# A causal convolution and a low-rank mixer: batch 0 in four half-row pieces, another warm-up, and one convolution a piece later

## The chip, the cores and the metric

The kernel runs on one core of a Trainium2 chip. A core has five engines that run side by side, each through its own queue in order: TensorE (PE, matrix products, with its weight loads shown as PEld), VectorE (DVE), ScalarE (ACT), GpSimd (POOL) and SyncE (SP). Matrix products land in PSUM, eight banks of 128 partitions x 512 float32 values; everything else lives in SBUF. Sixteen DMA engines move data between memory and SBUF.

The metric is the device time of one execution in microseconds. Before the change it is 331.23 us, the median of five runs (330.65 to 331.52).

## The reference

Eight batches of 4224 positions with 192 channels go through a causal convolution of 7 taps (softmax weights, one set for each of 8 heads of 24 channels), and then through a mixer: a rank-32 product over the positions is added, and a two-layer network over the channels with 768 hidden values is added to that.

```python
w = np.exp(weight - np.max(weight, axis=-1, keepdims=True))
w = w / (np.sum(w, axis=-1, keepdims=True) + 1e-09)
x_pad = np.concatenate([np.zeros((B, K - 1, D)), x], axis=1)
x_unf = x_pad[:, idx, :].reshape(B, S, K, H, group)      # idx = s + k
y = np.einsum('hk,bskhg->bshg', w, x_unf).reshape(B, S, D)

h = y.transpose(0, 2, 1) @ U @ V                         # over positions, rank 32
u = y + h.transpose(0, 2, 1)
out = u + np.maximum(u @ w_ch1, 0.0) @ w_ch2
```

## The kernel before

**Tiles.** The positions of a batch are 33 tiles of 128. x is held in blocks of 64 positions: partitions 0 to 63 (r = 0) hold the first 32 blocks, partitions 64 to 127 (r = 1) the last 34. The loads of x convert float32 to bfloat16 on the way and are issued by GpSimd (`x_part`, L76 to L82). The convolution is a matrix product with a band matrix: `conv` (L368) multiplies blocks of x by `band` (L181), two products for each block (itself and the block before), in 64 x 64 corners of the array, so that up to four run at once. It writes PSUM, and ACT (for r = 0) and DVE (for r = 1) copy the result to `y_sb` as bfloat16 (`evac`, L270 to L274). For batches 2 and later `conv32` (L334) does it with 32-row corners, and needs a copy of x shifted by 32 positions, `xb_sb`, that GpSimd makes in six steps (`x_shift`, L299 to L330).

**The head.** The band is built on the chip: GpSimd writes index tables (`iota`, L103 to L123), DVE makes a one-hot table `hot` of them, ACT and DVE the softmax weights `c_sb`, DVE the product `pr` of both (L223), in two halves of four heads, PE sums the seven taps through an identity (L231), and ACT copies the sums into `band` (L240). Meanwhile x of batch 0 is on its way in two pieces, each of both halves: `KP` (L86) cuts the tiles of each half at 13. PE runs 60 idle matmuls of zeros at the start and 30 ahead of the conv (`idle`, L170 and L688). Then PE does, in this order (L688 to L704): the conv of piece 0, head by head; `u_layout` (L276), which brings U into the order of the tiles with a selection matrix `Eq` and leaves `U_sb`; the transposes of y for the first group (`yT_part`, L542); the rank products of the first 26 tiles (`tt_mm`, L405, in four columns of 32 of the array); the conv of piece 1; a float32 product that adds up the four columns (`R4f`, L701); the rank products of the seven late tiles, each with U repeated four times, `U4_sb`, which DVE copies (L435); `tt_done` (L459), DVE's copy of the sum to `tt_sb`; `hT_part` (L558), which adds h to the transposed y and gives `uT`; and the first layer of the network, `w1` (L582, matmul in L590).

**The order of the rest.** Nothing is scheduled by a planner: each engine runs in the order in which the program is written, and a tile's reuse puts in the waits. `SLOTS` (L642 to L679) lists, slot by slot, which groups of eight tiles go through `w1` (36 matmuls each) and `w2` (L608, four pieces of 12 matmuls each), and ahead of which piece of `w2` the other work is put: `c3:0:3` is the conv of batch 3 for heads 0 to 2, `x4:3` the first three steps of the shifted copy of batch 4, `t3` the rank products of batch 3, `s3` their sum, `h10` group 10's mixer addition and transpose. For batches 3 and later the conv stands ahead of pieces 1, 2 and 3 (L669 to L671). The loads of batches 2 and later are held back until a given matmul of `w1` (`LOADS`, L682, `held`, L631).

**GpSimd's queue.** GpSimd issues all loads but one, in the order in which they are written: the first piece of x, index tables, U, the second piece, V for the first group, W1 in four parts, V in five, W2, x of batch 1, and then the four copies that make `band2` (L712). The completion signals of its loads go round over eight semaphores, so from the ninth load on an issue waits for the landing of the load eight before it. The first loads of x are the first two, U the next two, the second piece the fifth and sixth.

Of the kernel before, what the change touches and what calls it, by code (L numbers as in the profile page):

```python
# [7 lines left out]
ALU = mybir.AluOpType  # L8
# [6 lines left out]
def kernel(  # L15
# [10 lines left out]
    nc = tc.nc  # L26
# [59 lines left out]
    KP = [(0, 13), (13, NB1 // 2)]  # L86

    def x_piece(k):
        for r in range(2):
            k0, k1 = KP[k]  # L90
            k1 = min(k1, (NB0, NB1)[r] // 2)
            x_part(0, r, (1 - r if k == 0 else 2 * k0 + 1), 2 * k1 + 1)

    x_tile(0)
    x_piece(0)
# [5 lines left out]
    dif = cst.tile([P, BW], F32, name="dif")  # L101
    for r in range(4):
        nc.gpsimd.iota(  # L103
            dif[QB * r : QB * r + QB, :],
            pattern=[[1, BW]],
            base=0,
            channel_multiplier=-1,
            allow_small_or_imprecise_dtypes=True,
        )
    tap = cst.tile([P, KC], F32, name="tap")  # L110
    nc.gpsimd.iota(
        tap[:],
        pattern=[[-1, KC]],
        base=HW,
        channel_multiplier=0,
        allow_small_or_imprecise_dtypes=True,
    )

    fp = cst.tile([P, P], I32, name="fp")
    nc.gpsimd.iota(fp[:], pattern=[[1, P]], base=P, channel_multiplier=-1)  # L120

    efp = cst.tile([P, 4, P], I32, name="efp")
    nc.gpsimd.iota(efp[:], pattern=[[-1, 4], [1, P]], base=4 * P, channel_multiplier=-4)  # L123
# [11 lines left out]
    x_piece(1)  # L135


    V0_sb = cst.tile([32, 2 * GT * P], BF16, name="V0_sb")
# [28 lines left out]
    zz = cst.tile([P, 512], BF16, name="zz")  # L167
    nc.vector.memzero(zz[:])  # L168

    def idle(n, w):  # L170
        wps = bank()
        for _ in range(n):
            nc.tensor.matmul(  # L173
                out=wps[:, 0:w], lhsT=zz[:, 0:P], rhs=zz[:, 0:w], start=True, stop=True
            )

    idle(60, P)
# [3 lines left out]
    band = cst.tile([P, H, P], BF16, name="band")  # L181
    nc.vector.memzero(band[:])
    x_zero(0, nc.vector)
    hot = cst.tile([P, KC, BW], BF16, name="hot")
    nc.vector.tensor_tensor(
        out=hot[:],
        in0=dif[:].unsqueeze(1).to_broadcast([P, KC, BW]),
        in1=tap[:].unsqueeze(2).to_broadcast([P, KC, BW]),
        op=ALU.is_equal,
# [11 lines left out]
    nc.scalar.activation(e_sb[:], d_sb[:], ACT.Exp)  # L201
    ident = cst.tile([P, P], BF16, name="ident")
# [16 lines left out]
    HQ = H // 2  # L219

    def band_half(hh):
        pr = sml.tile([P, KC, HQ, BW], BF16, name="pr")
        nc.vector.tensor_tensor(  # L223
            out=pr[:],
            in0=hot[:].unsqueeze(2).to_broadcast([P, KC, HQ, BW]),
            in1=c_sb[:, :, HQ * hh : HQ * hh + HQ].unsqueeze(3).to_broadcast([P, KC, HQ, BW]),
            op=ALU.mult,
        )
        bp = bank()
        for d in range(KC):  # L230
            nc.tensor.matmul(  # L231
                out=bp[:, 0 : HQ * BW],
                lhsT=ident[:],
                rhs=pr[:, d, :, :],
                start=(d == 0),
                stop=(d == KC - 1),
            )
        for r in range(4):
            o = QB * (r % 2)
            nc.scalar.activation(  # L240
                out=band[QB * r : QB * r + QB, HQ * hh : HQ * hh + HQ, o : o + BW],
                in_=bp[QB * r : QB * r + QB, 0 : HQ * BW].rearrange("p (h t) -> p h t", h=HQ),
                func=ACT.Copy,
            )

    band_half(0)
    band_half(1)


    Eq = cst.tile([P, 4, P], BF16, name="Eq")  # L250
    nc.vector.tensor_scalar(
        out=efp[:], in0=efp[:], scalar1=P - 1, scalar2=None, op0=ALU.bitwise_and
    )
    nc.vector.tensor_scalar(
        out=Eq[:], in0=efp[:], scalar1=0.0, scalar2=None, op0=ALU.is_equal
    )
    nc.vector.tensor_scalar(
        out=fp[:], in0=fp[:], scalar1=R - 1, scalar2=None, op0=ALU.bitwise_and
    )
    R4f = cst.tile([P, P], F32, name="R4f")  # L260
    nc.vector.tensor_scalar(
        out=R4f[:], in0=fp[:], scalar1=0.0, scalar2=None, op0=ALU.is_equal
    )
    R4 = cst.tile([P, P], BF16, name="R4")
    nc.vector.tensor_copy(out=R4[:], in_=R4f[:])

# [9 lines left out]
    def u_layout():  # L276
        up = [bank() for _ in range(4)]
# [11 lines left out]
        for jj in range(4):  # L289
            evac(  # L290
                "AD"[jj % 2],
                U_sb[:, 0 : nb[jj], jj, :],
                up[jj][:, 0 : nb[jj] * R].rearrange("p (k r) -> p k r", r=R),
            )

# [38 lines left out]
    def conv32(b, h0, nh, engs):  # L334
# [5 lines left out]
        for n in range(nh):  # L340
# [3 lines left out]
            for cg in range(4):  # L344
                t, w, st = (
                    (xt[b], band[:, h, QB : 2 * QB], 1 + cg // 2)
# [21 lines left out]
    def conv(b, h0, nh, rs, engs, k0=0, k1=NT):  # L368
# [4 lines left out]
        pp = {r: bank() for r in rs}  # L373
        w = nh * GS
        for hh in range(nh):
            h = h0 + hh
            for halo in range(2):
                for r in rs:
                    for c in range(2):
# [5 lines left out]
                            lhsT=band[HB * r : HB * r + HB, h, HB * halo : HB * halo + HB],  # L385
# [42 lines left out]

    def tt_first(p, js, rest):


        U4_sb = cst.tile([P, sum(b - a for a, b in rest), 4, R], BF16, name="U4_sb")
        n = 0
        for a, b in rest:
            nc.vector.tensor_copy(  # L435
                out=U4_sb[:, n : n + b - a, :, :],
                in_=U_sb[:]
                .rearrange("p k j r -> p (k j) r")[:, a:b, :]
                .unsqueeze(2)
                .to_broadcast([P, b - a, 4, R]),  # L440
            )
            n += b - a
        p = tt_mm(0, js, p, 256)
        t = sml.tile([P, D], F32, name="tt_f", bufs=1)
        evac("A", t[:], p[:, 256 : 256 + D])
        return U4_sb, t

    def tt_more(p, U4_sb, rest):
        js = [j for a, b in rest for j in range(a, b)]
        for n, j in enumerate(js):  # L450
            nc.tensor.matmul(
                out=p[:, 0:D],
                lhsT=U4_sb[:, n, :, :].rearrange("p a r -> p (a r)"),
                rhs=yt[0][:, j, :],
                start=False,
                stop=(n + 1 == len(js)),
            )
# [84 lines left out]
    def yT_part(g):  # L542

        tp = [bank() for _ in range(3)]
        for c in range(3):
# [12 lines left out]
    def hT_part(g, tp, engs):  # L558

        uTt[g] = uts.tile([P, 4, 3, P], BF16, name="uT")  # L560
        for c in range(3):
            for hf in range(2):
                nc.tensor.matmul(
                    out=tp[c][HB * hf : HB * hf + HB, :],
                    lhsT=ttb[0][0:32, HB * c : HB * c + HB],
# [4 lines left out]
                )  # L570
            for n, eng in enumerate(engs):
# [90 lines left out]
    for k in range(5, 14):  # L662
# [3 lines left out]
        if k < 10:  # L666
# [21 lines left out]
    idle(30, P)  # L688
    for h in range(H):
        conv(0, h, 1, [0, 1], "AD", *KP[0])  # L690
    u_layout()
    yT = yT_part(0)
    jb = NB0 // 2
    rest = [(KP[1][0], jb), (jb + KP[1][0], NT)]
    ps0 = bank()
    U4_sb, tf = tt_first(
        ps0, list(range(KP[1][0])) + list(range(jb, jb + KP[1][0])), rest
    )
    for h in range(0, H, 4):
        conv(0, h, 4, [0, 1], "AD", *KP[1])  # L700
    nc.tensor.matmul(out=ps0[:, 0:D], lhsT=R4f[:], rhs=tf[:], start=True, stop=False)  # L701
    tt_more(ps0, U4_sb, rest)
# [7 lines left out]
    for r in range(4):  # L710
        q = slice(QB * r, QB * r + QB)
        nc.gpsimd.tensor_copy(  # L712
            out=band2[q], in_=band[q, :, HB * (r % 2) : HB * (r % 2) + QB]
        )
# [84 lines left out]
```

## Time and profile before

| what | value |
|---|---|
| median of five runs | 331.23 us (330.65 to 331.52) |
| the profiled execution | 331.23 us, its span 329.4 us |
| PE busy | 317.9 us, 97% of the span |
| DVE busy | 268.6 us, 82% |
| ACT busy | 170.9 us, 52% |
| POOL busy | 142.0 us, 43% |
| idle matmuls L173 | 90, 6.9 us busy |
| W1 matmuls L590 | 1188, 132.0 us busy |
| W2 matmuls L614 | 1584, 141.7 us busy |
| conv matmuls L381 of x 64x312 (piece 0) | 64, starting 11.43 to 15.3 us |
| first matmul of W1 | at 21.68 us |

All times in the profile are in microseconds from the start of the span, means of one instruction in nanoseconds. A line of the timeline gives start, length, engine, line of the program, operation, what is written and read, its shape, how many instructions were merged, and in brackets how long the engine was idle before and what ended the wait. Matmuls overlap, so a busy PE may still be waiting for part of the time; PEclk is the clock that a throttle granted, which was 1.00 through the span.

### The profile page before, as it was taken

Reading aid. Unit: us, or ns where it says so; the run is one execution under the profiler, and the core shown is the slowest. Engines: PE = TensorE matmul, PEld = TensorE weight load, DVE = VectorE, ACT = ScalarE, POOL = GpSimd, SP = SyncE. Lnnn points to the kernel's source line nnn. Section 1 sums busy time; section 2 is a strip of 40 time slices with the busy share of each in tenths; the row PEclk is TensorE's granted clock in tenths of the full one; section 3 lists DMA queues with packets and bytes.
Section 4 is the critical chain, followed back from the end, with each engine's and each line's share of the span. In section 5 each row is a group of like instructions: output and inputs, shape, how many; then the busy total and the mean of one; then the engine's idle time right before and its main releaser. Section 6 shows DMA issues by size and latency. Waiting matters only on the chain.

```text
span 329.4 us, 9736 instructions
## 1 busy us (share of the span) xinstructions
PE 317.9 (97%) x4072; PEld 223.8 (68%) x4072; DVE 268.6 (82%) x547; ACT 170.9 (52%) x351; POOL 142.0 (43%) x109
## 2 busy tenths in 40 slices
PE   6889999999999999999999999999999999999995
PEld 6655676567646845976874694587797487487495
DVE  5657999996985998798699789879897897896863
ACT  1658444563486098258619806842912912912910
POOL 8580229763995695969559599000000000000000
PEclk9999999999999999999999999999999999999999
DMA  8999995799999999799989969039659159249035
GB/s 100 192 167 167 158 213 144 143 190 178 240 194 182 163 173 190 172 223 195 183 192 191 182 160 224 19 105 237 76 113 277 45 128 240 67 115 270 1 123 169
DMA packets 122908, 53.54 MB, mean 163 GB/s; under 512 B 87760, under 2 KB 122832, under 8 KB 122864
## 3 DMA queue, kind: packets, MB, share of 16 engines
q1 hardware_dynamic: 84672, 38.18, 51.0%
q0 software_dynamic: 38192, 14.73, 39.3%
q8 instruction: 32, 0.52, 0.7%
q14 instruction: 12, 0.10, 0.1%
HBM read 29.49 MB, written 25.95 MB: 168 GB/s over the span
## 4 chain that ended last, share of the span: by engine, by line
PE 78%; POOL 8%; DMA 7%; DVE 3%; ACT 3%; issue 1%; POOLq 0%; DVEq 0%
PE ps L614 37%; PE ps L590 32%; DMA x_sb<-in_x_dram 7%; POOL xb_sb L318 5%; PE ps L352 3%; PE ps L496 3%; ACT rl_sb L601 2%; POOL x_sb L79 2%; PE ps L411 2%; DVE y_sb L274 2%; POOL xb_sb L306 1%; DVE rl_sb L603 1%; PE ps L381 0%; PE ps L467 0%; DVE uT L274 0%
## 5 line engine op out<-in xcount | busy, mean ns | idle before, releaser
L601 ACT ACTIVATE rl_sb<-ps 128x512 bf16<-128x512 f32 x235 | 125.3, 605 | 111.1 <-PE ps L590 107.8
L614 PE MATMUL ps<-W_sb,rl_sb 128*128 128x192 bf16 x1584 | 141.7, 247 | 0.2
L614 PEld LDWEIGHTS <-rl_sb 128*128 128x128 bf16 x1584 | 128.0, 98 | 13.4 <-issue 12.8
L590 PE MATMUL ps<-uT,W_sb 64*128 64x512 bf16 x1188 | 132.0, 377 | 0.8 <-DVE uT L274 0.8
L603 DVE TENSOR_SCALAR rl_sb<-ps 128x512 bf16<-128x512 f32 x161 | 104.3, 687 | 17.7 <-PE ps L590 17.4
L590 PEld LDWEIGHTS <-W_sb 64*128 64x128 bf16 x1188 | 64.3, 94 | 64.2 <-issue 5.0
L622 DVE TENSOR_TENSOR out_sb<-ps,u_sb 128x384 f32<-128x384 f32 (+1 forms) x133 | 70.1, 549 | 24.9 <-PE ps L614 24.5
L318 POOL COPY xb_sb<-x_sb 32x3072 bf16<-32x3072 bf16 (+1 forms) x24 | 67.6, 2824 | 0.7
L518 DVE TENSOR_TENSOR u_sb<-y_sb,ps 128x192 bf16<-128x192 bf16 (+1 forms) x168 | 66.2, 459 | 0.0
L306 POOL COPY xb_sb<-x_sb 128x3072 bf16<-128x3072 bf16 x12 | 32.7, 2742 | 30.0 <-PE ps L352 15.9
L272 ACT ACTIVATE y_sb<-ps 128x384 bf16<-128x384 f32 (+3 forms) x90 | 36.8, 503 | 10.9 <-PE ps L352 7.9
L79 POOL DMA_DIRECT2D x_sb<-in_x_dram x32 | 27.0, 851 | 27.2 <-PE ps L590 16.2
L274 DVE CAST y_sb<-ps 128x408 bf16<-128x408 f32 (+2 forms) x42 | 20.8, 547 | 4.1 <-PE ps L381 3.0
L496 PE MATMUL ps<-tt_sb,V_sb 32*128 32x192 bf16 x264 | 12.6, 247 | 0.8 <-DVE tt_sb L461 0.6
L352 PE MATMUL ps<-xb_sb,band 64*32 64x384 bf16 (+1 forms) x192 | 12.4, 332 | 0.8 <-POOL xb_sb L318 0.8
L352 PE MATMUL ps<-x_sb,band 64*32 64x384 bf16 x192 | 12.1, 333 | 0.0
L496 PEld LDWEIGHTS <-V_sb 32*128 32x128 bf16 x264 | 4.7, 92 | 8.2 <-issue 8.2
L352 PEld LDWEIGHTS <-band 64*32 64x32 bf16 x384 | 4.6, 90 | 5.2 <-issue 4.1
L381 PE MATMUL ps<-x_sb,band 64*64 64x312 bf16 (+3 forms) x192 | 7.2, 277 | 0.9 <-DMA x_sb<-in_x_dram 0.9
L173 PE MATMUL ps<-zz 128*128 128x128 bf16 x90 | 6.9, 251 | 1.2 <-DVE zz L168 1.2
L425 ACT ACTIVATE tt_hi<-ps 128x192 bf16<-128x192 f32 x7 | 2.3, 330 | 10.8 <-PE ps L411 10.8
L173 PEld LDWEIGHTS <-zz 128*128 128x128 bf16 x90 | 6.6, 116 | 1.2 <-DVE zz L168 1.2
(64 smaller groups left out, 71.9 us busy)
## 6 DMA issues: line engine op xcount, KB each, us to landing
out_dram<-out_sb SPq DMA_DIRECT2D x131, 192.0 KB, 2.9
x_sb<-in_x_dram POOLq DMA_DIRECT2D x14, 384.0 KB, 7.3
x_sb<-in_x_dram POOLq DMA_DIRECT2D x7, 432.0 KB, 7.7
x_sb<-in_x_dram POOLq DMA_DIRECT2D x7, 408.0 KB, 7.8
x_sb<-in_x_dram POOLq DMA_DIRECT2D x1, 648.0 KB, 10.2
x_sb<-in_x_dram POOLq DMA_DIRECT2D x1, 624.0 KB, 7.3
uT<-u_sb SPq DMA_TRANSPOSE x31, 4.4
W_sb<-in_moe_w_ch_dram POOLq DMA_DIRECT2D x2, 192.0 KB, 5.2
```

Of the source, the lines that this page charges most:

```text
L79: return nc.gpsimd.dma_start(out=xt[b][HB * r : HB * r + HB, s0:s1, :], in_=x[b, blk * HB : (blk + s1 - s0) * HB, :].rearrange("(j p) d -> ...
L272: nc.scalar.activation(out=out, in_=in_, func=ACT.Copy)
L274: nc.vector.tensor_copy(out=out, in_=in_)
L306: nc.gpsimd.tensor_copy(out=xbt[b][:, s0:s1, :], in_=xt[b][:, s0 + 1 : s1 + 1, :])
L318: nc.gpsimd.tensor_copy(out=xbt[b][q, s0:s1, :], in_=xt[b][q, s0:s1, :])
L352: nc.tensor.matmul(out=pp[r][QB * cg : QB * cg + QB, 0 : nk[r] * GS], lhsT=w[hr], rhs=t[hr, st : st + 2 * nk[r] - 1 : 2, hs], start=True, ...
L518: nc.vector.tensor_tensor(out=u_group(g)[:, i : i + n, :, hf, :], in0=yt[b][:, run[0] : run[0] + n, :].rearrange("p n (c k) -> p n c k", c=3),
L590: last = nc.tensor.matmul(out=pp[hf][:], lhsT=W1_sb[HB * hf : HB * hf + HB, c, m * P : (m + 1) * P], rhs=uTt[g][HB * hf : HB * hf + HB, :, ...
L601: nc.scalar.activation(out=rl[:, m, hf, :], in_=pp[hf][:], func=ACT.Relu)
L603: nc.vector.tensor_scalar_max(out=rl[:, m, hf, :], in0=pp[hf][:], scalar1=0.0)
L614: nc.tensor.matmul(out=cps[:, a * D : (a + 1) * D], lhsT=rlt[g][:, m, hf, (i + a) * P : (i + a + 1) * P], rhs=W2_sb[:, m, :], start=(m == ...
L622: nc.vector.tensor_tensor(out=o[:, 0:n, :].rearrange("p n (c k) -> p n c k", c=3), in0=cps[:, 0 : n * D].rearrange("p (n c k) -> p n c k", ...
```

## The change

It has four parts.

1. Batch 0 comes in four pieces of one half each: tiles 0 to 9 of the half r = 0, tiles 0 to 9 of r = 1, then r = 1 from 10 (7 tiles), then r = 0 from 10 (6 tiles). The first two go through the conv together, two heads at a time; the third and fourth by themselves, three heads at a time, into the four PSUM banks that `u_layout` used.
2. The warm-up is six idle matmuls of float32 and 512 columns (five at the start, one between the two band halves) in place of ninety of bfloat16 and 128 columns.
3. Both products `pr` of the band are made ahead of both sums, the band lies in two tiles, DVE copies the second half of it, the index tables are made with one `iota` each and per-quarter offsets `rq` that DVE adds, and `Eq` is made in one step. `U4_sb` and `R4` are copied by GpSimd, behind all issues of loads and ahead of x of batch 1; `band2` is made by eight copies. The rank products of the first 20 tiles come after the conv of the third piece, the transposes of y in columns 128 to 191 after the late rank products, and `hT_part` issues all its matmuls ahead of its copies.
4. In the slot of batch 3 the conv and what follows it (`x4:3`, `t3`, `s3`) stand one piece of `w2` later.

The diff, cut to its core:

```diff
-    KP = [(0, 13), (13, NB1 // 2)]
+    KP = [(0, 0, 10), (1, 0, 10), (1, 10, NB1 // 2), (0, 10, NB0 // 2)]
     def x_piece(k):
-        for r in range(2):
-            k0, k1 = KP[k]
-            k1 = min(k1, (NB0, NB1)[r] // 2)
-            x_part(0, r, (1 - r if k == 0 else 2 * k0 + 1), 2 * k1 + 1)
+        r, k0, k1 = KP[k]
+        x_part(0, r, (1 - r if k0 == 0 else 2 * k0 + 1), 2 * k1 + 1)
...
-    x_piece(0)
+    for k in range(2):
+        x_piece(k)
...
-    for r in range(4):
-        nc.gpsimd.iota(dif[QB * r : QB * r + QB, :], pattern=[[1, BW]], ...)
+    iota(dif[:], [[1, BW]], 0, -1)
...
-    x_piece(1)
+    for k in range(2, len(KP)):
+        x_piece(k)
...
-    zz = cst.tile([P, 512], BF16, name="zz")
+    zz = cst.tile([P, 512], F32, name="zz")
     nc.vector.memzero(zz[:])
+    rq = cst.tile([P, 2], F32, name="rq")
+    for r in range(4):
+        for n, v in enumerate((32.0, -128.0)):
+            nc.vector.memset(rq[QB * r : QB * r + QB, n : n + 1], v * r)
-    idle(60, P)
+    wps = bank()
+    def idle(n):
+        for _ in range(n):
+            nc.tensor.matmul(out=wps[:], lhsT=zz[:, 0:P], rhs=zz[:], start=True, stop=True)
+    idle(5)
...
+    nc.vector.tensor_scalar(
+        out=dif[:], in0=dif[:], scalar1=rq[:, 0:1], scalar2=None, op0=ALU.add
+    )
...
-        for r in range(4):
-            o = QB * (r % 2)
-            nc.scalar.activation(out=band[...], in_=bp[...], func=ACT.Copy)
+        for r in range(4):
+            o = QB * (r % 2)
+            evac("AD"[hh], bands[hh][...], bp[...])
     band_half(0)
+    idle(1)
     band_half(1)
...
-    idle(30, P)
-    for h in range(H):
-        conv(0, h, 1, [0, 1], "AD", *KP[0])
-    u_layout()
-    yT = yT_part(0)
-    ps0 = bank()
-    U4_sb, tf = tt_first(
-        ps0, list(range(KP[1][0])) + list(range(jb, jb + KP[1][0])), rest
-    )
-    for h in range(0, H, 4):
-        conv(0, h, 4, [0, 1], "AD", *KP[1])
-    nc.tensor.matmul(out=ps0[:, 0:D], lhsT=R4f[:], rhs=tf[:], start=True, stop=False)
-    tt_more(ps0, U4_sb, rest)
+    for h in range(0, H, 2):
+        conv(0, h, 2, [0, 1], "AD", *KP[0][1:])
+    work = [bank() for _ in range(4)]
+    u_layout(work)
+    o = 0
+    for js in late:
+        nc.gpsimd.tensor_copy(
+            out=U4_sb[:, o : o + len(js), :, :],
+            in_=U_sb[:]
+            .rearrange("p k j r -> p (k j) r")[:, js[0] : js[-1] + 1, :]
+            .unsqueeze(2)
+            .to_broadcast([P, len(js), 4, R]),
+        )
+        o += len(js)
+    nc.gpsimd.tensor_copy(out=R4[:], in_=R4f[:])
+    ps0 = bank()
+    yT = yT_part(0, (0, 1))
+    conv_piece(2, work[0:3])
+    tt_mm(0, piece_tiles(0) + piece_tiles(1), ps0, 256)
+    tf = sml.tile([P, D], F32, name="tt_f", bufs=1)
+    evac("A", tf[:], ps0[:, 256 : 256 + D])
+    conv_piece(3, [work[3], work[0], work[1]])
+    nc.tensor.matmul(out=ps0[:, 0:D], lhsT=R4f[:], rhs=tf[:], start=True, stop=False)
+    tt_late(ps0, late[0], 0, False, False)
+    tt_late(ps0, late[1], len(late[0]), False, True)
+    yT_part(0, (2,), yT)
     tt_done(0, ps0)
     hT_part(0, yT, "AD")
...
-        if k < 10:
+        if k == 5:
+            at = {
+                2: ["c3:0:3:AAD"],
+                3: ["c3:3:3:AAD"],
+                4: ["c3:6:2:A", "x4:3"],
+                5: [hs[0]],
+                6: ["t3"],
+                8: ["s3", hs[1]],
+                11: [hs[2]],
+            }
+        elif k < 10:
```

`late` holds the tiles of the third and fourth piece (26 to 32, then 10 to 15), and `tt_late` is the loop of `tt_more` for one of them.

## The prediction

> **What bounds the kernel now.** I read the page first, then the chain of waits in order of time, then the timeline of GpSimd (POOL) and of TensorE (PE), and last the waits of PE. The chain over the whole span says that PE is the bound:
>
> ```profile
> PE 78%; POOL 8%; DMA 7%; DVE 3%; ACT 3%; issue 1%; POOLq 0%; DVEq 0%
> ```
>
> The rest of the chain lies in two places, and the change touches both. One is the head, the first 22 us, up to the first W1 matmul (L590). The chain there (start, length, what):
>
> ```profile
> 2.38 10.23 DMA x_sb<-in_x_dram
> 12.65 0.47 PE ps L381 x6
> 13.14 2.44 DVE y_sb L274 x6
> ...
> 19.07 0.77 PE ps L451 x7
> ...
> 19.93 0.37 DVE tt_sb L461
> ...
> 20.35 0.42 PE ps L563 x2
> ...
> 21.68 1.08 PE ps L590 x6
> ```
>
> The first load of x holds everything to 12.65, then eight casts on VectorE (DVE), the rank products, `tt_sb` at 19.93, and the first W1 matmul at 21.68. From there PE runs with hardly a gap, so what the head gains or loses at `tt_sb` arrives at the end one to one. The other place is the conv of batch 3, where PE stands still once more, for GpSimd's last shifted copy, which ends at 99.41 (PE's timeline, then GpSimd's):
>
> ```profile
> 99.46 0.33 PE L352 MATMUL ps<-xb_sb,band 64*32 64x408 bf16 x1 [0.83 <-POOL xb_sb L318]
> ```
> ```profile
> 96.33 3.08 POOL L318 COPY xb_sb<-x_sb 32x3456 bf16<-32x3456 bf16 x1
> ```
>
> **Own time.** The profiled execution took 331.23 us, the median of the five runs; its span is 329.4, so 1.83 lie around it. I add changes to 331.23.
>
> **The conv of batch 3 a piece later.** One W2 piece more stands ahead of it on PE: twelve matmuls, 1.10 us on the chain. PE reached the conv at 98.30 and sat 0.83 from its second matmul on; with 1.10 ahead it arrives at 99.40 and finds the copy done at 99.41, so about 0.8 goes, leaving 0 to 0.05. PE and GpSimd both shift with the head, since GpSimd's chain is anchored on PE's held-back load at 61.78 (after 1.57 of waiting), so the relation holds. What is moved along: `x4:3`, `t3`, `s3`. The shifted copies of batch 4 may start when conv 3 ends, 103.53 before and about 103.5 after, and GpSimd then waits 3.21 us for PE at 115.88 anyway; that wait covers a piece. `t3` to `s3` stays two pieces apart, and the next group after `s3` (h11) is all batch 2. Cost nothing.
>
> **The head until the conv.** x_tile 0 now comes as 20, 21, 14 and 12 blocks in four loads instead of 26, 27, 6 and 8. The data rate is steady at 188 to 194 GB/s from 5 us on, in order of issue: the first two loads together (1272 KB) landed at 12.6; now they are 984 KB, 288 KB or 1.55 us less, so about 10.9 (a shorter descriptor issue gives 0.15 more). One iota instead of four saves some 0.6 us of GpSimd, the band no longer waits for it: DVE's products `pr` (1.26 us each) end near 6.9 and 8.1 instead of 7.93 and 9.15, in spite of eight memsets of `rq` (0.1 each at most) and a `zz` of twice the size (0.49 by the band's row, not 0.27). DVE evacuates the second band half (four at about 0.28, after ACT's 288 ns row) and makes `Eq`; both lie before 11.5. The conv of pieces 0+1 is four evacuations on each of ACT and DVE (480 elements, about 0.58 and 0.65, between the rows of 384 and 512), not eight of 312, so 2.6 on DVE for 3.21.
>
> Idle matmuls: before, 90 of bf16. The windows of their line alone show what they do:
>
> ```profile
> 3.00:4.00 1.00, 1.00 (x12) 1.00 (x11) 1.00 0.75 54
> 4.50:5.50 1.00, 1.00 (x21) 1.00 (x20) 1.00 1.52 177
> ```
>
> The columns are time, PE and weight-load busy with counts, PEclk, DMA. PEclk says 1.00 throughout, but the number of 128-column matmuls in a microsecond doubles after 4.3. So PE starts at half pace (about 107 ns each) and opens 3.1 us after the first matmul. No float32 matmul of this size is in the trace; L701 (192 columns) gives 0.52 us on the chain for its two halves, 1.4 for 512. [...]
>
> PE's line then: conv 10.9 to 12.6, u_layout held by DVE's second cast to 12.9 and done at 13.4, `U_sb` out at about 14.9, third piece 14.1 to 15.3 (its load lands near 14.0), 20 rank matmuls to 15.95, fourth piece (load at 15.7) to 17.0, R4f to 17.4. **Were that all, the thirteen late rank matmuls (81 ns each) would end at 18.75 and `tt_sb` begin at 18.85 instead of 19.93: 1.1 saved.**
>
> The other reorderings cost nothing there: `hT_part` issues its six matmuls before its evacuations, which wait for the same two matmuls as before; the third and fourth piece write into the four banks of u_layout, whose evacuations are counted above.
>
> **What is late next: U4_sb.** It moved from DVE (L435, 352 and 282 ns) to GpSimd, and in GpSimd's order it comes after all load issues, the W2 weights' included. GpSimd before:
>
> ```profile
> 14.77 1.13 POOL L153 DMA_DIRECT2D V_sb<-in_moe_V_dram  x2
> 16.12 1.08 POOL L153 DMA_DIRECT2D V_sb<-in_moe_V_dram  x2 [0.22 <-issue]
> 17.19 0.58 POOL L160 DMA_DIRECT2D V_sb<-in_moe_V_dram  x1
> 17.76 0.86 POOL L164 DMA_DIRECT2D W_sb<-in_moe_w_ch_dram  x1
> 18.61 0.21 POOL L74 MEMSET x_sb<- 64x96 uint32 x1
> ```
>
> The third V issue (16.12) reuses the semaphore of the last x load, so it waits for that landing (issued at 7.35, 8.5 us, 15.85). x and U are the same bytes in total as before, at the same rate, so that landing stays, 0.15 earlier at best. Then four issues: 0.54+0.54+0.58+0.86 = 2.52. GpSimd is free at 18.45, as it was at 18.62. The copies then are 128 x 896 and 128 x 768. Their price by the nearest rows:
>
> ```profile
> L306 POOL COPY xb_sb<-x_sb x12: 2742/2742/2745, 48.1 to 190.8; 128x3072 bf16<-128x3072 bf16 x12
> L308 POOL COPY xb_sb<-x_sb x6: 500/500/501, 54.0 to 193.6; 32x384 bf16<-32x384 bf16 x6
> L712 POOL COPY band<-band x4: 386/393/398, 22.2 to 23.5; 32x256 bf16<-32x256 bf16 x4
> ```
>
> From 384 to 3072 elements the slope is 0.83 ns, with 0.18 fixed (256 gives 0.39, which fits): 0.93 and 0.82. [...] At DVE's rate (0.634 us for 896 elements, 0.71 ns) the pair would be 1.2; by the rows 1.75. I take the rows: same engine, same dtype, only the four-fold repeat is new. So the second copy is ready at 18.45+1.75+0.08 = 20.3 (20.0 with DVE's rate and an early landing, 20.6 with 10% more for the repeat).
>
> PE works seven late matmuls on the first copy from 19.45, waits, and does the last six from 20.4: 0.73 (7 took 0.81), ends 21.1, `tt_sb` at 21.2 instead of 19.93. **The head is 1.2 us longer, from 0.9 to 1.6**, not 1.1 shorter. Behind the waiting late matmuls on PE lie the transposes of the third 64 columns (8 matmuls, 0.3, which fit under the `tt_sb` cast of 0.36), hT and W1. After `tt_sb` the steps to W1 are the same, so W1 starts at 22.9.
>
> On GpSimd, R4 (about 0.3) and x of batch 1 are queued behind the copies: its four issues start at 20.6 instead of 18.73, and eight band2 copies of 0.29 take the place of four of 0.39, so it ends near 26.5 instead of 24.1. Its next issue waited for PE until 32.69 (8.56 idle), so that is covered; batch 1's loads, 8 us each, land by 32 and are used at 41.15. SP's queue has nothing new.
>
> PE's new idle stretch, 17.4 to 19.45, is 2.0 us. The longest in the trace that kept the full pace is 1.77 (6.26 to 8.03; band matmuls of 152 columns then took 67 ns each). [...] If it fell, the 0.83 of hT and 4.3 of W1 would cost some 1.5; I take zero.
>
> **Sum**: 331.23 + 1.2 - 0.8 = 331.6, with 0.9 to 1.6 and 0.75 to 0.83: 331.3 to 332.1. A measurement can tell about 0.2%, 0.66 us, from no change, so the likeliest case is within it: the head's gain is eaten by a copy in a queue, and the conv's gain pays most of that back.
>
> **Rivals.** *The copy is not the bound* (chance 0.11): GpSimd gets through its issues two microseconds sooner, because the last load lands sooner or its wait falls away. Against it: same bytes, same rate, an issue order that puts the copies last. Then 331.23 - 1.1 - 0.8 = 329.3. *The clock does not open* (0.08): float32 zeros are no activity for the gate. [...] It decides as soon as PE's line is more than 2.2 late, the slack under the copy; slower, 331.23 + 3.4 - 0.8 = 333.8. For it: no float32 stream is in the trace; against: zeros in bf16 did open it. *The batch 3 wait stays* (0.08), because GpSimd slips with its longer list: 331.23 + 1.2 = 332.4; against it stand the 8.56 and 1.57 of slack. The likeliest has 0.73.
>
> **Chances and range.** Likeliest 0.73, of which 0.58 within 0.2%, 0.13 above, 0.02 below. Slower: 0.13 + 0.08 + 0.08 = 0.29; faster 0.02 + 0.11 = 0.13; same 0.58. The range from 330.0 to 332.8 takes in the likeliest and the third rival and leaves out 0.19.
>
> **What would show it.** The two U4 copies on GpSimd start near 18.5 and end near 20.3, straight after the W2 issue; PE's late matmuls wait for GpSimd twice, some 2 us and then 0.4; `tt_sb` near 21.2, first W1 near 22.9. First conv matmul of the second half near 10.9. No wait for xb_sb at the conv of batch 3, and W1 to end 0.8 shorter. I am wrong if the copies end before 18, if conv starts after 13, or if the end moves by another amount than `tt_sb` less 0.8.

## The result, and the profile after

The changed kernel takes 331.73 us, the median of 43 runs (330.15 to 335.07), beside 331.08 us for the kernel before in 80 runs. The medians are 0.65 us apart; the ratio worked out from all runs is 1.0024, 95% interval 1.0009 to 1.0038, so the loss is small but clear of no change. The forecast of 331.6 was 0.13 below the median.

The profiled execution of the changed kernel tells another story than the median: it took 330.61 us (span 328.8), which is 0.62 *less* than the profiled execution of before. Its chain of waits in the head, in order of time (start, length, what):

```profile
1.47 7.29 PE ps L174 x10
...
10.12 0.48 PE ps L237 x7
...
10.62 0.30 DVE band L259
...
11.96 0.48 DVE Eq L286
...
12.89 1.23 DVE y_sb L259 x2
...
18.25 0.52 PE ps L717 x2
18.77 0.62 PE ps L682 x7
...
19.40 0.69 PE ps L682 x6
...
20.18 0.37 DVE tt_sb L437
...
21.93 1.08 PE ps L568 x6
```

`tt_sb` starts at 20.18, where before had 19.93, and the first W1 matmul at 21.93 instead of 21.68: the head is 0.25 us longer, not 1.2. Ahead of the late rank matmuls (L682) no wait of GpSimd's is left on the chain. The load queue and the two `U4_sb` copies stand in GpSimd's timeline (the copies write `U4_sb` from `U_sb`; the trace calls both U_sb):

```profile
15.05 1.19 POOL L149 DMA_DIRECT2D V_sb<-in_moe_V_dram  x2 [0.98 <-DMA x_sb<-in_x_dram]
16.23 0.52 POOL L156 DMA_DIRECT2D V_sb<-in_moe_V_dram  x1
16.73 0.88 POOL L160 DMA_DIRECT2D W_sb<-in_moe_w_ch_dram  x1
17.66 1.69 POOL L701 COPY U_sb<-U_sb 128x896 bf16<-128x896 bf16 x2
```

The order is the one forecast: third V issue held by x, then the issues, then the copies, 1.69 us for the pair (forecast 1.75). But the third V issue comes at 15.05, where before had 16.12, so the copies start at 17.66, not 18.45. PE on the other hand is late: five float32 idle matmuls end at 8.76. The second half of the band is therefore summed only by 10.6, DVE's copies of it and DVE's `Eq` end at 12.4 (forecast 11.5), and DVE's casts of `y_sb`, for which `u_layout` waits, start at 12.89; so PE reaches the late rank matmuls at 18.6 (forecast 17.4). The weight loads show how little it then waits, in brackets, for each of the copies:

```profile
18.64 0.53 PEld L682 LDWEIGHTS <-U_sb 128*128 128x128 bf16 x7 [0.16 <-POOL U_sb L701]
19.40 0.45 PEld L682 LDWEIGHTS <-U_sb 128*128 128x128 bf16 x6 [0.24 <-POOL U_sb L701]
```

The second place is the conv of batch 3, first in PE's timeline, then in GpSimd's:

```profile
97.45 2.15 PE L592 MATMUL ps<-W_sb,rl_sb 128*128 128x192 bf16 x24
99.54 0.35 PE L355 MATMUL ps<-xb_sb,band 64*32 64x384 bf16 x2
```
```profile
81.09 2.74 POOL L309 COPY xb_sb<-x_sb 128x3072 bf16<-128x3072 bf16 x1 [3.17 <-DMA x_sb<-in_x_dram]
...
95.40 3.08 POOL L321 COPY xb_sb<-x_sb 32x3456 bf16<-32x3456 bf16 x1
```

The conv starts without a wait, as forecast. But its shifted copy ended at 98.48, 0.93 earlier than before, because the chain of copies hangs on the landing of x of batch 3 (3.17 us of waiting), not on PE. Without the move PE would have come to the conv 1.10 earlier, at 98.44, and would have waited for next to nothing. The sum of the profiled execution closes: 331.23 + 0.25 (head) - 0.83 (wait gone) = 330.65, measured 330.61.

So the profile has a gain of 0.6 and the median a loss of 0.65. What separates them is in the list of all executions, each with its mean granted clock of TensorE:

| executions | clock 0.997 and up | 0.991 to 0.996 | below 0.991 |
|---|---|---|---|
| before (39 runs beside the first experiments) | 26, median 330.65 us | 13, 332.29 us | none |
| after (43 and the profiled one) | 25, 330.61 us | 7, 332.64 us | 12, 334.11 us |

At full clock the medians of the two kernels are 0.04 us apart. The means of all these executions are 331.18 and 332.02; without those below 0.991, of which the kernel before has none, the mean of after is 331.24. So nearly the whole difference, 0.8 on the mean, comes from them. The experiments ask where and why the clock falls.

### The profile page after: what moved, and what is told of

Its sections match the earlier page's. It is cut to its first block, busy times and chain, and to the rows that moved or that the text cites. A ratio compares the mean times of both kernels' runs of the same rounds, so it can differ in the third digit from the quotient of the medians.

```text
span 328.8 us, 9589 instructions
## 1 busy us (share of the span) xinstructions
PE 320.3 (97%) x3994; PEld 221.1 (67%) x3994; DVE 269.2 (82%) x553; ACT 170.4 (52%) x345; POOL 144.0 (44%) x113
## 4 chain that ended last, share of the span: by engine, by line
PE 91%; DVE 5%; ACT 3%; issue 0%; DVEq 0%
PE ps L592 41%; PE ps L568 37%; PE ps L355 3%; PE ps L472 3%; PE ps L174 2%; ACT rl_sb L579 2%; PE ps L417 2%; DVE y_sb L259 1%; DVE rl_sb L581 1%; PE ps L385 1%; DVE u_sb L494 1%; PE ps L682 0%; DVE out_sb L600 0%; DVE band L259 0%; PE ps L443 0%
## 5 line engine op out<-in xcount | busy, mean ns | idle before, releaser
L581 DVE TENSOR_SCALAR rl_sb<-ps 128x512 bf16<-128x512 f32 x161 | 104.4, 687 | 17.7 <-PE ps L568 17.4
L257 ACT ACTIVATE y_sb<-ps 128x384 bf16<-128x384 f32 (+4 forms) x88 | 37.4, 512 | 10.7 <-PE ps L355 7.8
L259 DVE CAST y_sb<-ps 128x408 bf16<-128x408 f32 (+4 forms) x38 | 20.2, 578 | 1.6 <-PE ps L385 1.5
L355 PE MATMUL ps<-xb_sb,band 64*32 64x384 bf16 x192 | 12.1, 332 | 0.0
L174 PE MATMUL ps<-zz 128*128 128x512 f32 x12 | 8.4, 855 | 1.5 <-DVE zz L164 1.5
L385 PE MATMUL ps<-x_sb,band 64*64 64x240 bf16 (+3 forms) x192 | 8.0, 276 | 0.4 <-DVE band L259 0.4
L385 PEld LDWEIGHTS <-band 64*64 64x64 bf16 x192 | 6.0, 106 | 2.2 <-issue 1.2
```

The source lines that it names most:

```text
L257: nc.scalar.activation(out=out, in_=in_, func=ACT.Copy)
L355: nc.tensor.matmul(out=pp[r][QB * cg : QB * cg + QB, 0 : nk[r] * GS], lhsT=w[hr], rhs=t[hr, st : st + 2 * nk[r] - 1 : 2, hs], start=True, ...
L581: nc.vector.tensor_scalar_max(out=rl[:, m, hf, :], in0=pp[hf][:], scalar1=0.0)
```

## Experiments

Three things were to be told apart. *The copy*: `U4_sb` in GpSimd's queue holds the late matmuls, and PE's wait there lets the clock fall. *The warm-up*: six float32 matmuls are a thin warm-up, and the clock falls for that. *The slot*: the move of the conv is worth 0.8. Each ratio is to runs of the kernel before on the same chip; their median was 330.94 us for the first four experiments, 331.06 for the next three, and 330.78 for the last, which ran on another chip.

### The changed kernel once more

No edit.

> The changed kernel unchanged. The profiled execution was 0.6 us shorter than the one of before, yet the median of its runs is 0.65 us longer, and its runs with a mean granted clock of 0.999 lie near 330.4 to 331.9 while those with 0.994 and 0.988 lie near 332.6 and 334.1. Theory 'clock': the difference is made by executions in which PE's clock falls back; they show again as a group near 332.6 and one near 334.1, about half of all, and a profile of one would show PEclk below 1 for 3.5 or 7 us somewhere in the first 30 us. Theory 'copy': every execution is longer by the wait for U4_sb; then the times form one group near 331.7.

Measured: 332.84 us (22 runs, 330.32 to 335.08), ratio 1.0044 (1.0018 to 1.0069). Ten executions at clock 0.997 and up have a median of 330.71, the three from 0.991 to 0.996 one of 332.85, and the nine below 0.991 one of 334.09. The three groups are the same as in the table above to 0.2 us; the median alone moves with the share of the groups (here it falls on the small middle group). The profiled execution was again one at full clock (0.997, span 328.6), with the copies at 17.57.

### The changed kernel with the warm-up of before

```diff
-    zz = cst.tile([P, 512], F32, name="zz")
+    zz = cst.tile([P, 512], BF16, name="zz")
...
-            nc.tensor.matmul(out=wps[:], lhsT=zz[:, 0:P], rhs=zz[:], start=True, stop=True)
+            nc.tensor.matmul(
+                out=wps[:, 0:P], lhsT=zz[:, 0:P], rhs=zz[:, 0:P], start=True, stop=True
+            )
-    idle(5)
+    idle(60)
...
     band_half(0)
-    idle(1)
     band_half(1)
+    idle(30)
```

> The changed kernel with the warm-up of before: 60 idle matmuls of bfloat16 at the start and 30 between the band and the conv. Theory 'clock': the low-clock groups go or shrink to what before has, and the median falls by about 1 us below the changed kernel's, to 330.2 to 330.7. Theory 'copy': the late rank matmuls wait for the same copies, so the same median as the changed kernel within 0.4 us.

Measured: 333.68 us (10 runs), ratio 1.0071 (1.0040 to 1.0101). Seven of ten executions are below 0.991; the other three have a median of 332.0. The theory of the warm-up falls: with the fuller warm-up the clock falls more often, not less. PE's and GpSimd's timelines of this profile (335.23 us, clock 0.984), then windows over all its lines (time, length, busy and count of PE, PEld, DVE, ACT, POOL, then the granted clock, DMA share, GB/s):

```profile
17.06 0.59 PE L719 MATMUL ps<-tt_f,R4f 128*128 128x192 f32 x2
19.26 2.26 PE L684 MATMUL ps<-y_sb,U_sb 128*128 128x192 bf16 x13 [1.61 <-POOL U_sb L703]
```
```profile
15.79 1.08 POOL L149 DMA_DIRECT2D V_sb<-in_moe_V_dram  x2 [1.77 <-DMA x_sb<-in_x_dram]
18.28 1.70 POOL L703 COPY U_sb<-U_sb 128x896 bf16<-128x896 bf16 x2
```
```profile
17.00:18.00 1.00, 0.65 (x7) 0.30 (x2) 0.59 (x1) 0.48 (x2) 1.00 (x2) 1.00 1.27 194
18.00:19.00 1.00, 0.00 (x0) 0.00 (x0) 0.00 (x0) 0.00 (x0) 0.96 (x2) 0.90 1.42 193
19.00:20.00 1.00, 0.74 (x5) 0.71 (x6) 0.00 (x0) 0.00 (x0) 1.00 (x3) 0.50 0.80 61
...
28.00:29.00 1.00, 1.00 (x8) 0.35 (x5) 0.04 (x1) 0.81 (x3) 0.00 (x0) 0.50 1.61 193
29.00:30.00 1.00, 1.00 (x12) 0.43 (x8) 0.66 (x1) 0.82 (x2) 0.00 (x0) 0.98 1.66 207
```

PE arrives earlier here (R4f, the float32 product that adds up the four columns, at 17.06 instead of 18.18), finds no `U4_sb`, because the third V issue waited for x until 15.79, and stands still from 17.65 to 19.26. It is an idle stretch like the one of 2.0 us that the prediction had drawn for the changed kernel. The granted clock halves at about 18.8 (0.90 in the window from 18 to 19 is full pace for 0.8 of it), 1.15 us after the last matmul ended, and stays at half until 29.0, for 10.2 us. The thirteen late matmuls take 2.26 us for 1.43, the six of `hT_part` 1.48 for 0.83, the first 36 W1 matmuls 6.7 for 4.3. From the start of the first to the end of the last it is 11.1 us, beside 7.6 in the kernel with PE kept busy below, whose clock held: 3.5 more. This execution is 3.2 above the median of the three at full clock (335.23 and 332.0).

### The kernel before with the float32 warm-up

```diff
-    zz = cst.tile([P, 512], BF16, name="zz")
+    zz = cst.tile([P, 512], F32, name="zz")
...
-    idle(60, P)
+    idle(5, 512)
...
-    idle(30, P)
+    idle(1, 512)
```

> The kernel before with five float32 idle matmuls at the start and one ahead of the conv, in place of 60 and 30 of bfloat16. Theory 'clock': the median rises by 1 us or more over before, through executions with a granted clock of 0.994 and 0.988. Theory 'copy': the conv waits for x until 12.6 us anyway, which hides the longer idles; the same as before within 0.4 us.

Measured: 335.15 us (6 runs, 333.63 to 337.72), ratio 1.0141 (1.0094 to 1.0189). Its two executions at full clock have 333.8, where before has 330.65, so most of the loss is not the clock. In the profile (333.91 us, clock 0.999) the first loss is in PE's timeline, ahead of the late rank matmuls:

```profile
20.45 0.67 PE L451 MATMUL ps<-y_sb,U_sb 128*128 128x192 bf16 x6 [1.37 <-issue]
```

"issue" is a wait for nothing that the profile shows. In the same stretch, 18 to 20 us, lies the first packet of 16 KB of the instruction queue q8, which every kernel here with a bf16 warm-up has at 12 to 14 us (before at 13.44). That q8 is PE's queue and that PE ran out of instructions is read from this coincidence and not tested by itself. By the first W1 matmul the profile is 1.30 behind that of before. It loses another 0.96 in the 108 W1 matmuls ahead of the conv of batch 3 (12.79 us for 11.83, with no wait shown; why stays open), and 0.29 at that conv, where PE waits 1.12 for `xb_sb` and before 0.83: 2.55 of the 2.68 between the two profiles. So the two warm-ups can't be exchanged alone in either kernel.

### The kernel before with the slot move alone

```diff
-        if k < 10:
+        if k == 5:
+            at = {
+                2: ["c3:0:3:AAD"],
+                3: ["c3:3:3:AAD"],
+                4: ["c3:6:2:A", "x4:3"],
+                5: [hs[0]],
+                6: ["t3"],
+                8: ["s3", hs[1]],
+                11: [hs[2]],
+            }
+        elif k < 10:
```

> The kernel before with the conv of batch 3 one W2 piece later and nothing else. All theories: the wait of 0.83 us for xb_sb goes, 0.7 to 0.9 us faster than before (ratio 0.9973 to 0.9979), whatever the clock does. If the wait stays or comes back at another conv: the same as before.

Measured: 330.42 us (14 runs), ratio 0.9989 (0.9965 to 1.0013), so not clear of no change; at full clock 330.27 beside 330.65, 0.4 less, where 0.7 to 0.9 was expected. The profile has no wait for `xb_sb` at the conv; the copy ended at 98.61 (95.53 + 3.08) and PE came at 98.90:

```profile
95.53 3.08 POOL L318 COPY xb_sb<-x_sb 32x3456 bf16<-32x3456 bf16 x1
```
```profile
98.90 0.35 PE L352 MATMUL ps<-xb_sb,band 64*32 64x384 bf16 x2
```

### U4_sb on VectorE

```diff
     for js in late:
-        nc.gpsimd.tensor_copy(
+        nc.vector.tensor_copy(
             out=U4_sb[:, o : o + len(js), :, :],
```

> The changed kernel with the two copies of U4_sb on VectorE again, at the same place of the program, so no longer behind the load issues. PE's line reaches the late rank matmuls at 18.6 in the changed kernel's profile, just as the first copy ends, so at full clock only 0.2 to 0.4 us are to be had (330.2 to 330.5). Theory 'copy wait closes the clock': the group with a mean granted clock of 0.988 (0.43 of the changed kernel's executions are below 0.997) goes, and the median falls by 1 us or more. Theory 'the thin warm-up closes the clock': the low-clock share stays near 0.4 and the median within 0.5 us of the changed kernel's.

Measured: 329.86 us (22 runs, 328.89 to 330.65), ratio 0.9954 (0.9937 to 0.9971). All 22 executions have a clock of 0.997 and up. The low-clock group is gone, as the theory of the copy expected. At full clock the gain is also larger than expected, 0.75 (330.61 to 329.86) for 0.2 to 0.4, and the profiles don't show where all of it lies: `tt_sb` starts at 20.00 here, only 0.18 earlier, in an execution that is itself above its median (330.33). DVE's timeline, PE's and GpSimd's:

```profile
16.06 0.95 DVE L701 COPY U_sb<-U_sb 128x896 bf16<-128x896 bf16 x2
```
```profile
18.23 0.59 PE L717 MATMUL ps<-tt_f,R4f 128*128 128x192 f32 x2
18.66 1.24 PE L682 MATMUL ps<-y_sb,U_sb 128*128 128x192 bf16 x13
21.75 1.49 PE L568 MATMUL ps<-uT,W_sb 64*128 64x512 bf16 x10 [0.51 <-DVE uT L259]
```
```profile
18.31 0.86 POOL L160 DMA_DIRECT2D W_sb<-in_moe_w_ch_dram  x1 [1.49 <-DMA W_sb<-in_moe_w_ch_dram]
```

The copies lie at 16.06 to 17.01, and the late matmuls follow R4f without a bracket. The last line matters too: here GpSimd sat 1.49 us, at the issue of W2's load, for the landing of a part of W1, the load eight before it, because the signals of its loads go round over eight semaphores (99 to 106 in the traces of the kernels before and after; in both, W2's issue waits on 99, which W1's second part has). Behind that wait stood only `R4`, the loads of batch 1 and `band2`, and no wait of PE's in the head is for them. In the changed kernel `U4_sb` stands behind it.

### U4_sb on VectorE, and the warm-up of before

The two edits above together.

> The changed kernel with the warm-up of before and U4_sb on VectorE. With the copies on GpSimd this warm-up brought PE to the late matmuls at 17.6 and then 1.6 us of waiting, and 7 of 10 executions had a clock of 0.988 or less. Theory 'copy wait': no wait now, tt_sb near 19.0 instead of 20.1, full-clock executions at 329.3 to 329.8, the low-clock group at most as frequent as before's (13 of 39): median 329.5 to 330.3, faster than both kernels. Theory 'thin head': PE has fewer idle matmuls than before and gaps of its own, so the clock still falls in half of the executions, median 331 or more.

Measured: 329.62 us (11 runs, 329.06 to 330.37), ratio 0.9943 (0.9921 to 0.9964), all at a clock of 0.997 and up. This is the lowest median here, 1.44 us below before; the 0.24 to the kernel of the previous section is too little to tell the two apart. Its late matmuls start at 18.06 and the first W1 matmul at 21.15, 0.5 earlier than in before:

```profile
21.15 2.13 PE L570 MATMUL ps<-uT,W_sb 64*128 64x512 bf16 x16 [0.51 <-DMA V_sb<-in_moe_V_dram]
```

The bracket names a load of V, but the same 0.51 stands in the previous kernel, put down to `uT`, and `uT` is what this matmul reads; so the wait is for `uT`, and no load of weights is shown to be the next bound.

The bf16 warm-up, harmful with `U4_sb` on GpSimd (333.68), does no harm without it. That is the plainest evidence that the copy's place is the cause and the warm-up is not.

### The bf16 warm-up, U4_sb on GpSimd, and PE kept busy

On top of the second experiment, 28 more idle matmuls of 64 columns ahead of R4f, which only occupy PE:

```diff
     conv_piece(3, [work[3], work[0], work[1]])
+    for _ in range(28):
+        nc.tensor.matmul(
+            out=ps0[:, 448:512], lhsT=zz[:, 0:P], rhs=zz[:, 0:64], start=True, stop=True
+        )
     nc.tensor.matmul(out=ps0[:, 0:D], lhsT=R4f[:], rhs=tf[:], start=True, stop=False)
```

> The changed kernel with the warm-up of before, U4_sb on GpSimd, and 28 idle matmuls of 64 columns (about 1.5 us) ahead of the R4f product, so PE works where it waited for U4_sb. They delay nothing while the copy is late. Theory 'the idle stretch closes the clock': the clock stays, 0.988 goes from 7 of 10 to at most 2 in 10, the median falls from 333.7 to about 332.0 (the full-clock executions without the filling lay at 331.7 to 332.3). Theory 'something else closes it' (load of the loads, the conv's half-empty array): the low-clock share stays at 0.7 and the median near 333.7.

Measured: 331.44 us (22 runs, 331.08 to 331.94), ratio 1.0004 (0.9989 to 1.0019). All but one of the executions have a clock of 0.997 and up, the last 0.996. PE's timeline:

```profile
17.30 0.99 PE L720 MATMUL ps<-zz 128*128 128x64 bf16 x28
18.13 0.57 PE L723 MATMUL ps<-tt_f,R4f 128*128 128x192 f32 x2
19.34 1.43 PE L684 MATMUL ps<-y_sb,U_sb 128*128 128x192 bf16 x13 [0.64 <-POOL U_sb L703]
```

The copies come as late as without the filling (18.35 and 18.28), the late matmuls too (19.34 and 19.26), only the stretch without a matmul is 0.64 for 1.61. The median is 2.2 us lower (333.68 to 331.44), and the executions below 0.991, seven of ten before, are gone. At full clock the two differ by 0.6 (332.0, of three executions, and 331.44), so some 1.7 of the 2.2 is the clock. So without matmuls in this stretch the clock falls in seven of ten executions, and with them none of 22 is below 0.996; whether it is the shorter gap or the added work that counts, this run can't separate. Of the 1.82 left above the kernel with the copies on DVE, 1.48 is the copies' own lateness: `tt_sb` at 20.88 for 19.4.

### Three more profiles of the changed kernel

No edit; each a single profiled execution, in the hope of one whose clock falls.

> The changed kernel again for one more profile. With a chance of 0.43 it is an execution with a low granted clock; then the theory that the wait for U4_sb closes it expects PEclk to fall to 0.5 between 18 and 20 us, after a stretch in which PE is idle waiting for GpSimd, and the other theory (thin warm-up) expects it to fall ahead of 15 us.

> The changed kernel for one more profile, in the hope of one with a low granted clock (chance 0.43). Theory 'the copy wait closes the clock': PEclk falls to 0.5 between 18 and 20 us after PE has been idle for the copies, for 3.4 to 10 us. Theory 'thin warm-up': it falls ahead of 15 us.

> As after_look2: the changed kernel for one more profile. A low clock with its fall at 18 to 20 us behind a wait for U4_sb speaks for the copy wait, a fall ahead of 15 us for the thin warm-up; an execution at full clock says nothing.

The first had full clock (330.93 us, 0.997; copies at 17.47, PE without a wait). The other two, on another chip, had not: 334.5 us at 0.989 and 335.21 us at 0.984. GpSimd's timeline in the second profile, PE's, and the windows:

```profile
17.85 0.51 POOL L156 DMA_DIRECT2D V_sb<-in_moe_V_dram  x1 [1.51 <-DMA W_sb<-in_moe_w_ch_dram]
18.35 0.86 POOL L160 DMA_DIRECT2D W_sb<-in_moe_w_ch_dram  x1
19.25 1.70 POOL L701 COPY U_sb<-U_sb 128x896 bf16<-128x896 bf16 x2
```
```profile
20.24 1.43 PE L682 MATMUL ps<-y_sb,U_sb 128*128 128x192 bf16 x13 [2.67 <-POOL U_sb L701]
```
```profile
20.00:21.00 1.00, 0.75 (x7) 0.53 (x7) 0.00 (x0) 0.00 (x0) 1.00 (x3) 1.00 0.72 48
21.00:22.00 1.00, 1.00 (x14) 0.79 (x14) 0.22 (x1) 0.00 (x0) 1.00 (x3) 0.85 1.50 177
22.00:24.00 2.00, 1.91 (x12) 0.56 (x9) 0.85 (x3) 1.05 (x3) 2.00 (x4) 0.50 0.94 93
...
28.00:29.00 1.00, 1.00 (x10) 0.52 (x8) 0.08 (x1) 0.99 (x3) 0.00 (x0) 0.73 1.61 193
```

The third profile, GpSimd and PE:

```profile
17.46 0.51 POOL L156 DMA_DIRECT2D V_sb<-in_moe_V_dram  x1 [1.42 <-DMA W_sb<-in_moe_w_ch_dram]
18.86 1.69 POOL L701 COPY U_sb<-U_sb 128x896 bf16<-128x896 bf16 x2
```
```profile
19.85 2.26 PE L682 MATMUL ps<-y_sb,U_sb 128*128 128x192 bf16 x13 [1.82 <-POOL U_sb L701]
```

It has the same marks: the fifth V issue waits 1.42 us for W1's first part, the copies start at 18.86, and PE is idle for 1.82 us (18.03 to 19.85); there the clock halves near 19.2, after 1.2 us of idling, and is back near 29.5. In the second profile it holds through 2.67 us of idling, falls near 21.7, when PE has long been working again, and is back near 28.5. So the fifth V issue waits for an earlier load whose signal it takes over; in these two profiles, where that landing is late, the copies are 1.2 to 1.8 later, PE idles, and the clock falls. In the three profiles of this kernel without that wait (copies at 17.47, 17.57 and 17.66) PE waited for less than 0.3 at a time and the clock held.

The late copies are only one half of the stretch. The other is that PE comes early: by the traces' records of the granted clock, it opened at 4.64 and 5.56 us in these two executions, and R4f ended at 17.57 and 18.03; in the other three it opened at 5.84, 6.27 and 7.00, and R4f ended at 18.27, 18.41 and 18.77. With the copies at 17.66 these two would still have waited some 1.1 and 0.6 us (an estimate: their waits less the delay of their copies). Five profiles are few, but each step is seen in them. Why W1's first part lands later in some executions is not settled.

### U4_sb on VectorE, without the slot move

The fifth experiment, with the slot of batch 3 as before.

> The changed kernel with U4_sb on VectorE and with the conv of batch 3 where it was before (ahead of pieces 1, 2 and 3). With U4_sb on VectorE none of 22 executions had a low clock, so the conv's place can be weighed without it: that kernel's median is 329.86. If PE's wait for the last shifted copy comes back in full, this one is 0.8 us slower, 330.5 to 330.8, and PE shows a wait for xb_sb of 0.7 to 0.9 us at the conv of batch 3. If the loads of x land early enough by themselves, the wait is 0 to 0.3 and the median within 0.3 of 329.86.

Measured: 330.07 us (22 runs), ratio 0.9970 (0.9957 to 0.9983), beside 329.86 with the move. Both kernels ran at full clock throughout, but on different chips: against the kernel before on its own chip the move is worth more, 0.5 (0.9954 for 0.9970), so the figure is 0.2 to 0.5. This profile has no wait of PE's for `xb_sb` at the conv of batch 3 at all, though the conv stands where it stood before the change. GpSimd's timeline, then PE's:

```profile
80.06 2.74 POOL L309 COPY xb_sb<-x_sb 128x3072 bf16<-128x3072 bf16 x1 [2.01 <-DMA x_sb<-in_x_dram]
...
94.91 3.08 POOL L321 COPY xb_sb<-x_sb 32x3456 bf16<-32x3456 bf16 x1
```
```profile
98.68 0.35 PE L355 MATMUL ps<-xb_sb,band 64*32 64x384 bf16 x2
```

The copy ends at 97.99, ahead of PE. In before it ended at 99.41, in the kernel before with the other warm-up at 101.97. The landing of batch 3's second part, for which GpSimd waits at 80 to 84.5, moves by microseconds from profile to profile.

## Why the prediction was right in its number and wrong in most of its terms

**The cause named was the right one.** `U4_sb` queued behind GpSimd's load issues is what the change loses by: moved to DVE the same kernel is 1.87 us faster (331.73 to 329.86), and goes from 1.0024 to 0.9954 of before. But the way it loses is another than the one named: not by holding up every execution for a microsecond, but by letting the clock fall in some of them. The prediction's 1.1 for PE's line without the copy, with 0.8 for the slot, would have been 329.3; the kernel with the copies on DVE has 329.86.

**The head, +1.2 us: mis-sized, in both of its terms.** The prediction has PE idle from 17.4 and the copies from 18.45. The profiled execution has PE at 18.6 and the copies at 17.66, and the head +0.25. PE's term: its 1.1 saved needs the float32 idle matmuls to be out of the way before the conv at 10.9, and no run of before shows what one of 512 columns takes. The prediction's 1.4, from R4f's 0.52 us for 192 columns, met neither pace: in the changed kernel half a matmul took 0.855 us at half pace and 0.43 at full, so 1.71 and 0.86 for one. The clock opened 5.5 us after the first idle matmul, at 7.00, where before has 3.25, at 4.45; so the five ended at 8.76. The prediction also had DVE's copies of the second band half and `Eq` "before 11.5"; held back by that, they ended at 12.4 and carried the delay on to `u_layout`. GpSimd's term: "that landing stays, 0.15 earlier at best" was wrong by about a microsecond (15.05 for 16.12). With the bf16 warm-up the same order of loads has it at 15.79, so a good part hangs on the warm-up; the runs show no more than that (see the last section).

**Zero for the clock: this step failed.** For PE's idle stretch of 2.0 us the prediction took zero: a choice of the author's, which the trace of before, with 1.77 at the most, does not show. The stretch without a matmul ahead of the late matmuls was 1.61, 1.82 and 2.67 us in the three profiles whose clock fell, and the fall came after 1.15 us of idling at the least. The 1.5 that the prediction gave as the price of a fall no run shows either, and its own numbers don't give it: 0.83 of hT and 4.3 of W1 at half pace are 5.1 more; in the second experiment a fall cost 3.2. The clock stayed at half for 6.8 us once and 10.2 twice. In the median of the changed kernel this term, and not the head's +1.2, makes the loss.

**The slot, -0.8 us: the wait went, but the move was worth 0.2 to 0.5.** The step that failed is "GpSimd's chain is anchored on PE's held-back load at 61.78", "so the relation holds". A landing behind that anchor, near 81 us, sets the end of the copies: they ended anywhere from 97.97 to 99.41 in five profiles (the kernel before with and without the move, the changed kernel, and the two with the float32 warm-up and the copies on DVE) in which PE's first W1 matmul was within half a microsecond of before's. Before's profile happened to have the wait at 0.83. At full clock the move alone gives 0.4, and on top of the copies on DVE 0.2 to 0.5.

**The rivals.** *The copy is not the bound* is true of the profiled executions at full clock, nearly (0.16 and 0.24 of waiting), and false of the kernel. *The clock does not open* with float32 zeros: false, it opened in every profile with them, in those of the changed kernel at 4.64 to 7.00 us. The 3.4 in that rival's sum no run shows: the changed kernel's profile with the opening at 7.00 has the head 0.25 longer. *The batch 3 wait stays*: false.

**Taken together**, the sum of 331.6 came within 0.13 of the median by luck: terms that were wrong make up for each other. The prediction's +1.2 and -0.8 give +0.4. What the runs have in their place is about nothing at full clock (330.61 for 330.65: some +0.25 in the head, some -0.2 to -0.5 in the slot) and some +0.8 on the mean by the executions whose clock falls, a term that the prediction took at zero.

## What to carry to other kernels

When a copy moves to another engine, ask what stands ahead of it in that queue, load issues with their waits for reused signals included: here a wait of 1.49 us at W2's issue held nothing up with the copies on DVE, and waits of 1.42 and 1.51 us at the fifth V issue left PE idle for 1.82 and 2.67 us with the copies behind them. A PE wait of 1.61 us cost 3.2 us here by what the clock did after it, more than its length; move the cause of such a wait away (1.87 us off the changed kernel's median), or fill it with matmuls of zeros where the cause can't be moved (2.2 off with the bf16 warm-up). And look at the granted clock and time of all executions before trusting a single profile: here it showed a gain, and the median a loss.

## What the runs showed of the hardware that was not expected

- The granted clock fell to one half after 1.15 and 1.2 us without a matmul in two profiles, and in a third 1.5 us into the work that followed 2.67 us of it; it stayed there for 6.8 to 10.2 us, most of them full of work. By the traces' records of the clock the falls came 13.65, 13.65 and 17.07 us after it had opened, and the stays were 10.24, 10.24 and 6.83 us: all whole multiples of 3.41. So in these traces, once it was open, the clock changed only at the ends of stretches of 3.41 us, counted from its opening. In the stretch that ended in a fall PE had stood still for 1.14, 1.18 and 1.95 us. Yet in the kernel before, one with 1.60 us of standing still (6.26 to 7.86, the end of the first stretch after its clock opened at 4.45; the line below shows the whole gap) ended without a fall; what else counts is not settled.

```profile
8.03 0.62 PE L231 MATMUL ps<-pr,ident 128*128 128x152 bf16 x7 [1.77 <-DVE pr L223]
```

- The kernel before also falls below 0.997 in 40 of 113 executions (never below 0.991) and loses 1.6 us there (332.17 for 330.62), about what one stretch of 3.41 us at half pace would cost, 1.7 (an estimate; no profile here has caught one). The kernels with `U4_sb` on DVE never did in 55. What makes it fall in before is not settled.
- Float32 zeros opened the clock as bf16 zeros did. When it opened varied with both, and between executions of one kernel: by the records of the clock at 4.64 to 7.00 us in the five profiles of the changed kernel, and at 4.45 to 5.96 in the five kernels with bf16 zeros.
- With fewer idle matmuls a packet of instructions came later. The first 16 KB packet of the instruction queue q8, taken here for PE's, comes at 12 to 14 us in the five kernels with ninety idle matmuls or more, at 14 to 18 with six in the changed kernel, at 18 to 20 with six in the kernel before, where PE stood still for 1.37 us with nothing to wait for. The third V issue is at 14.8 to 15.2 in the seven profiles of the changed kernel with six, at 15.6 in the kernel before with six, and at 15.8 to 16.1 in the five with ninety: a coincidence over these profiles, not isolated.
- A copy of 128 x 896 bf16 elements with a four-fold repeat on the reading side took GpSimd no longer than a plain one (1.69 us for the pair, 1.75 worked out from plain rows); DVE took 0.89 to 1.19 for the same pair in three profiles.
